# State reads of an attention block: the product computed transposed at once

## The chip, the cores and the metric

The kernel runs on one core of a Trainium2 chip. The metric is the device time of one launch in microseconds (us), as the median of the runs. The core has a matrix engine (TensorE, PE in the profile; its weight loads are shown as a lane of their own, PEld), VectorE (DVE), ScalarE (ACT), GpSimd (POOL) and a queue that issues DMAs (SP).

## The reference, cut to what matters

```python
# x (8, 8, 512, 64), state (8, 8, 32, 64), all float32
scores2 = scale * np.matmul(state, x.transpose(0, 1, 3, 2))
a2 = softmax(scores2)                      # (8, 8, 32, 512)
sread = np.matmul(a2, x)                   # (8, 8, 32, 64): the state reads
xread = np.matmul(softmax(scale * x @ state^T), state)
h = concat([xread, sread], axis=2)         # then to (8 * 544, 512)
h = (sigmoid(h @ w_gate) * (h @ w_val)) @ w_out
out = np.square(np.maximum(h @ w_in, 0)) @ w_out2
```

The change is in how `sread` is made: for each batch and head, 32 rows of probabilities over 512 tokens times the head's 512 x 64 slice of x.

## The kernel before

Every float32 operand of a product is split into a high and a low part of type fp32r (`h` and `l`), and a product is the sum of high x high, high x low and low x high (`mm3`, lines 182 to 184). PSUM holds sums in float32.

The work falls into three stretches. In the first, weights are converted, the states are multiplied by the first layer's weights (`state_weights`, `ps_g`), and the scores and the probabilities of the token reads are made (part A of the attention, tiles `ps_s`, `a`). In the second, the first feed-forward layer runs over the tokens: 96 units, one for each block of 512 tokens and each 128 of the hidden features (`front_x` with `psg` and `psv`, `back1` with `acc`), and part B of the attention, the state reads, is woven into it. It closes with 12 units for the 256 state rows (`front_s`). In the third, the second layer runs (`px`, `py`, `pz`, `o`).

Part B goes over 8 batches and 2 groups `g` of 4 heads, so 16 groups. A group holds heads in pairs: index `c` (or `p`) and index `i`, 4 heads in all. Its steps are named: LN loads x by tokens (`xn`), LS loads the scores (`e2`), B4 makes the softmax, B5 transposes the probabilities to tokens on partitions and splits them into `et` (128 tokens, 4 blocks of tokens, c, high or low, 64 state rows of two heads), SX0 and SX1 split x into `xs` (ACT casts the high part, POOL subtracts), B60 and B61 multiply, and B7 brings the result to its place. The result has to lie in `xs_t` with features on partitions, since `split_states` (tile `sp`) and `front_s` read it that way.

In B60 and B61 the loaded operand is `et`: 4 matmuls, one for each block of 128 tokens, with 128 loaded columns (high and low of 64 state rows) and 256 streamed columns (high and low of two heads of x). The output has the high rows in partitions 0 to 63 and the low rows in 64 to 127. ACT copies the lower half to `tmp`, DVE adds the upper half and then adds the two parts of x into `sw`. When both halves of `sw` are there, B7 transposes it on PE (`ps_so`) and picks the 4 blocks of 64 x 32 that belong together, 2 by DVE and 2 by ACT, into `xs_t`.

The order is that of emission. `ORDER_B` lists part B's steps with blanks, and each batch's list is laid evenly over 5.4 units from unit 45 + 5b on (`spread(att_b[b], start, start + 5.4)`); `step()`, called 6 times in a unit, emits what is due. The order on each engine is then refined when the program is built, by readiness on a simulated timeline, so that steps can come out later than their place in the list. The pool `at` has two PSUM banks, for `ps_e`, `ps_sr`, `ps_so`, `ps_g` and `ps_s` in turn; `xs`, `xn`, `et` and `sw` have one buffer each.

Of the kernel before, what the change touches and what calls it, by code (L numbers as in the profile page):

```python
# [8 lines left out]
F32 = mybir.dt.float32  # L9
F32R = mybir.dt.float32r  # L10
# [8 lines left out]
P = 128  # L19
# [13 lines left out]
def kernel(  # L33
# [12 lines left out]
    nc = tc.nc  # L46
    B, H, S, D = x.shape
    NS = state.shape[2]
# [8 lines left out]
    NT = S // P  # L57
# [18 lines left out]
    at_p = ctx.enter_context(tc.tile_pool(name="at", bufs=2, space=PSUM))  # L76
# [13 lines left out]
    xs_t = xs_p.tile([P, KD, NSTATE], F32, name="xs_t")  # L90

    ident = pad_p.tile([P, P], F32, name="ident")
# [108 lines left out]
    f_p = att.enter_context(tc.tile_pool(name="f2k", bufs=2))  # L201
# [42 lines left out]
    loaded_x, loaded_xn = {}, {}  # L244
# [37 lines left out]
    def group_stages(b, g):  # L282

        v = {}
# [10 lines left out]
        def a2(p):  # L295
            def run():
                if by_pe:
                    xf = at_p.tile([P, S], F32, tag="at", name="ps_xt")
                    for t in range(NT):
                        ts = slice(t * P, (t + 1) * P)  # L300
                        nc.tensor.transpose(xf[:, ts], loaded_x[b, g][:, p, t, :], ident)
                else:
                    xf = f_p.tile([P, S], F32, tag="xf", name="xf", bufs=1)
                    nc.vector.transpose(xf, loaded_x[b, g][:, p, :])
                h = xx_p.tile([P, S], F32R, tag="xth", name="xth")
                l = xx_p.tile([P, S], F32R, tag="xtl", name="xtl")
                nc.scalar.copy(out=h, in_=xf)
                nc.vector.tensor_sub(out=l, in0=xf, in1=h.bitcast(F32))
                v["xt", p] = (h, l)

            return run
# [67 lines left out]
            )  # L379
            v["et"] = et  # L380

        def sx(p):
            def run():
                xn = loaded_xn[b, g][:, :, NT * p : NT * (p + 1), :]
                xs = f_p.tile([P, 2, 2, NT, D], F32R, tag="xs", name="xs", bufs=1)
                nc.scalar.copy(out=xs[:, 0], in_=xn)
                nc.gpsimd.tensor_sub(out=xs[:, 1], in0=xn, in1=xs[:, 0].bitcast(F32))
                v["xs", p] = xs

            return run  # L390

        def b6(p):
            def run():
                et, xs = v["et"], v.pop(("xs", p))
                ps = at_p.tile([P, 512], F32, tag="at", name="ps_sr")
                pv = ps[:, : 4 * D]
                for t in range(NT):
                    nc.tensor.matmul(
                        pv,
                        et[:, t, p].rearrange("p l n -> p (l n)"),  # L400
                        xs[:, :, :, t, :],
                        start=(t == 0),
                        stop=(t == NT - 1),
                    )
                tmp = f_p.tile([64, 2, P], F32, tag="tmp", name="tmp", bufs=1)
                if p == 0:
                    v["w"] = f_p.tile([P, P], F32, tag="sw", name="sw", bufs=1)
                sv = pv.rearrange("p (l m) -> p l m", l=2)
                nc.scalar.copy(out=tmp, in_=sv[64:128])
                nc.vector.tensor_add(out=tmp, in0=sv[:64], in1=tmp)  # L410
                nc.vector.tensor_add(
                    out=v["w"][64 * p : 64 * (p + 1)], in0=tmp[:, 0, :], in1=tmp[:, 1, :]
                )

            return run

        def b7():
            w = v.pop("w")
            ps = at_p.tile([P, 2, 64], F32, tag="at", name="ps_so")
            nc.tensor.transpose(ps.rearrange("p a b -> p (a b)"), w, ident)  # L420
            for p in range(2):
                for i in range(2):
                    to = xs_t[D * p : D * (p + 1), 2 * g + i, b * NS : (b + 1) * NS]
                    src = ps[D * i : D * (i + 1), p, NS * i : NS * (i + 1)]
                    if i:
                        nc.scalar.copy(out=to, in_=src)
                    else:
                        nc.vector.tensor_copy(to, src)

        return {  # L430
            "LX": lx, "LN": ln, "LS": ls, "A20": a2(0), "A21": a2(1), "A3": a3, "A4": a4, "SX0": sx(0), "SX1": sx(1),
            "B4": b4, "B5": b5, "B60": b6(0), "B61": b6(1), "B7": b7,
        }

    ORDER_A = "LX.0 - - - A20.0 A21.0 LX.1 A3.0 - A4.0 - A20.1 A21.1 A3.1 - A4.1".split()

    ORDER_B = (
        "LN.0 LS.0 - - - B4.0 SX0.0 - B5.0 LS.1 - B60.0 SX1.0 LN.1 - B61.0 B4.1 SX0.1 - B5.1 "
        "B7.0 - B60.1 SX1.1 - B61.1 - B7.1"
    ).split()  # L440

    def attention(b):
        gs = [group_stages(b, g) for g in range(2)]
        pick = lambda names: [
            (lambda: None) if n == "-" else gs[int(n[-1])][n[:-2]] for n in names
        ]
        return [lambda: prep_diag(b), *pick(ORDER_A)], pick(ORDER_B)
# [542 lines left out]
    for b in range(QB, B):  # L990
        start = 33 + 7 * (b - QB)
        spread(att_a[b], start, start + 7)
    for b in range(B):
        start = 45 + 5 * b
# [39 lines left out]
    for i, (b, f, lo, hi) in enumerate(units):  # L1034
        count[0] = STEPS * i
        g = (front_x if b < B else front_s)(b, f)
# [73 lines left out]
```

## Time and profile before

| | |
|---|---|
| Median of 3 runs | 1500.55 us (1496.91 to 2657.24) |
| Profiled execution | 1500.54 us, span 1498.8 us |
| PE busy | 1431.0 us, 95% of the span |
| DVE, ACT, POOL busy | 940.2, 748.8 and 246.0 us |
| Granted TensorE clock, mean | 0.985 of full speed |

The span goes from the first to the last instruction of the core; the profiled time has 1.7 us around it. Busy time is the union of an engine's instructions. Matmuls are pipelined: the shown duration of one is longer than its distance to the next, and it is the distance, from start to start, that fills the engine's time.

### The profile page before, as it was taken

The page shows a single profiled execution, that of the slowest core. Times are in us where ns is not written, and L with a number is a line of the kernel's source. Part 1 is how long each engine was busy: PE and PEld are TensorE (multiplying, and loading weights), DVE is VectorE, ACT ScalarE, POOL GpSimd, SP SyncE. Part 2 cuts the span into 40 slices and gives each one's busy share as a digit, 9 for nine tenths or more (in the row PEclk, how much of TensorE's full clock was granted, in tenths as well). Part 3 has the DMA queues.
Part 4 walks back from the last instruction along what each step waited for, and adds up shares of the span by engine and source line. Part 5 has one row for each costly group of instructions (what it writes and reads, how often), then busy time and mean ns, then how long its engine had stood idle before and what let it go on. Part 6 is the DMA issues. An engine that isn't in the chain of part 4 may idle for free.

```text
span 1498.8 us, 19379 instructions
## 1 busy us (share of the span) xinstructions
PE 1431.0 (95%) x6552; PEld 1176.9 (79%) x6552; DVE 940.2 (63%) x1579; ACT 748.8 (50%) x1291; POOL 246.0 (16%) x216
## 2 busy tenths in 40 slices
PE   5879999999999989999899999999999999999998
PEld 3558878887787677888798788888888888888887
DVE  7986887578889987555536655734575356433443
ACT  6865876456678887666424522332242223232211
POOL 1112213232344544333101100000000000000000
PEclk9889999999999999999999999999999999999999
DMA  9984799699999864333677844644365443645442
GB/s 265 341 263 120 229 328 339 210 363 292 323 296 286 254 211 145 95 113 92 242 271 250 274 158 147 217 146 143 133 227 188 151 152 134 222 124 195 155 145 80
DMA packets 244595, 311.68 MB, mean 208 GB/s; under 512 B 105361, under 2 KB 152977, under 8 KB 244497
## 3 DMA queue, kind: packets, MB, share of 16 engines
q1 hardware_dynamic: 242224, 309.66, 63.8%
q10 hardware_dynamic: 2272, 0.79, 0.3%
q8 instruction: 52, 0.85, 0.2%
q14 instruction: 47, 0.38, 0.1%
HBM read 221.25 MB, written 89.13 MB: 207 GB/s over the span
## 4 chain that ended last, share of the span: by engine, by line
PE 72%; DVE 10%; ACT 7%; DMA 7%; issue 3%; SPq 1%; POOL 0%; ACTq 0%; DVEq 0%; POOLq 0%
PE o L182 8%; PE o L183 8%; PE o L184 8%; PE px L183 4%; PE px L182 4%; PE px L184 4%; PE acc L183 4%; PE acc L184 3%; PE acc L182 3%; DMA raw<-in_moe_w_out_dram 2%; PE psg L182 2%; PE psg L183 2%; PE psg L184 2%; PE psv L182 2%; PE psv L183 2%
## 5 line engine op out<-in xcount | busy, mean ns | idle before, releaser
L182 PE MATMUL o<-wo,g2h 128*128 128x512 f32 x512 | 198.6, 390 | 3.7 <-DMA wo<-wo 3.0
L183 PE MATMUL o<-wo,g2h 128*128 128x512 f32 x512 | 199.1, 389 | 0.0
L184 PE MATMUL o<-wo,g2l 128*128 128x512 f32 x512 | 193.9, 389 | 0.0
L537 POOL TENSOR_TENSOR gg<-gi,gg 128x512 fp32r<-128x512 f32 x96 | 135.3, 1412 | 350.5 <-ACT gg L536 284.2
L183 PE MATMUL acc<-gl,o 128*128 128x512 f32 (+1 forms) x432 | 164.4, 381 | 3.7 <-DVE gl L190 3.7
L184 PE MATMUL acc<-gh,o 128*128 128x512 f32 (+1 forms) x432 | 163.0, 378 | 0.0
L841 ACT CAST g2h<-c 128x512 fp32r<-128x512 f32 x96 | 59.3, 622 | 178.8 <-DVE c L837 178.8
L182 PE MATMUL acc<-gh,o 128*128 128x512 f32 (+1 forms) x432 | 139.3, 380 | 0.6 <-DVE y L624 0.4
L893 DVE TENSOR_TENSOR y<-o,y 128x512 f32<-128x512 f32 x102 | 68.5, 688 | 103.5 <-PE o L184 102.8
L182 PEld LDWEIGHTS o<-wo,g2h 128*128 128x128 f32 x512 | 96.1, 188 | 24.9 <-ACT p L826 3.0
L184 PEld LDWEIGHTS o<-wo,g2l 128*128 128x128 f32 x512 | 96.1, 188 | 19.8
L183 PEld LDWEIGHTS o<-wo,g2h 128*128 128x128 f32 x512 | 96.2, 188 | 19.5
L190 DVE TENSOR_TENSOR gl<-g,gh 128x512 fp32r<-128x512 f32 (+1 forms) x108 | 88.4, 818 | 36.3 <-ACT gh L189 35.8
L182 PE MATMUL px<-xh,wi 128*128 128x512 f32 x256 | 99.8, 390 | 0.0
L183 PE MATMUL px<-xl,wi 128*128 128x512 f32 x256 | 99.7, 389 | 0.0
L184 PE MATMUL px<-xh,wi 128*128 128x512 f32 x256 | 99.6, 389 | 0.0
L183 PEld LDWEIGHTS acc<-gl,o 128*128 128x128 f32 x432 | 81.3, 188 | 21.3 <-DVE gl L190 6.9
L182 PEld LDWEIGHTS acc<-gh,o 128*128 128x128 f32 x432 | 80.6, 189 | 17.4 <-DVE y L624 1.1
L184 PEld LDWEIGHTS acc<-gh,o 128*128 128x128 f32 x432 | 81.3, 188 | 14.6
L182 PE MATMUL psg<-a,gg 128*128 128x512 f32 x192 | 78.6, 409 | 14.8 <-ACT sg L550 12.1
L556 DVE TENSOR_TENSOR g<-psv,sg 128x512 f32<-128x512 f32 x96 | 65.6, 683 | 35.4 <-PE psv L184 21.6
L189 ACT CAST gh<-g 128x512 fp32r<-128x512 f32 (+1 forms) x108 | 64.3, 596 | 40.4 <-DVE g L556 23.0
(188 smaller groups left out, 3268.7 us busy)
## 6 DMA issues: line engine op xcount, KB each, us to landing
wi<-wi SPq DMA_DIRECT2D x256, 256.0 KB, 3.1
wo<-wo SPq DMA_DIRECT2D x64, 512.0 KB, 5.5
gd<-go SPq DMA_DIRECT2D x192, 128.0 KB, 4.4
gi<-gd SPq DMA_DIRECT2D x96, 256.0 KB, 4.0
wi<-wa SPq DMA_DIRECT2D x32, 512.0 KB, 5.0
wd<-w SPq DMA_DIRECT2D x24, 512.0 KB, 5.1
ws<-wd SPq DMA_DIRECT2D x24, 512.0 KB, 6.7
raw<-in_moe_w_out_dram SPq DMA_DIRECT2D x20, 512.0 KB, 6.2
```

The lines of the kernel that those rows point to most:

```text
L182: nc.tensor.matmul(ps, lh, rh, start=start, stop=False, skip_group_check=more)
L183: nc.tensor.matmul(ps, lh, rl, start=False, stop=False, skip_group_check=more)
L184: nc.tensor.matmul(ps, ll, rh, start=False, stop=stop, skip_group_check=more)
L189: nc.scalar.copy(out=gh[:, :n], in_=g32[:, :n])
L190: nc.vector.tensor_sub(out=gl[:, :n], in0=g32[:, :n], in1=gh[:, :n].bitcast(F32))
L537: nc.gpsimd.tensor_sub(out=t[:, 1], in0=src, in1=t[:, 0].bitcast(F32))
L556: nc.vector.tensor_mul(out=g32, in0=ps, in1=sg)
L841: nc.scalar.copy(out=h, in_=c)
L893: nc.vector.tensor_add(out=y, in0=acc, in1=y)
```

## The change

B60 and B61 now go by `i` instead of `p`. The loaded operand is the split x (128 tokens x 128 columns: two heads `c`, 64 features each), once for its high and once for its low part, and `et` is streamed: 128 columns, which are c, high or low, and the 32 state rows of head `i`. A step so has 8 matmuls of 128 streamed columns in place of 4 of 256. High and low of x are summed in PSUM. The output has features on partitions, as `xs_t` wants it; of its columns, those of the other head `c` are not used. ACT copies the low columns of the probabilities to `tmp` (128 x 64), and DVE adds the high columns to it in two additions of 64 x 32 that write to `xs_t`. B7, with its transposition and its four copies, and the tile `sw` are gone. `tmp` has two buffers of 128 x 64 instead of one of 64 x 256. `xs` holds the same numbers in another order. `ORDER_B` loses its two B7 steps and a blank: 25 entries in place of 28, over the same 5.4 units.

```diff
-        def sx(p):
+        def sx(i):
             def run():
-                xn = loaded_xn[b, g][:, :, NT * p : NT * (p + 1), :]
-                xs = f_p.tile([P, 2, 2, NT, D], F32R, tag="xs", name="xs", bufs=1)
+                xn = loaded_xn[b, g][:, i].rearrange("p (c t) d -> p t c d", c=2)
+                xs = f_p.tile([P, 2, NT, 2, D], F32R, tag="xs", name="xs", bufs=1)
                 nc.scalar.copy(out=xs[:, 0], in_=xn)
                 nc.gpsimd.tensor_sub(out=xs[:, 1], in0=xn, in1=xs[:, 0].bitcast(F32))
...
-        def b6(p):
+        def b6(i):
             def run():
-                et, xs = v["et"], v.pop(("xs", p))
-                ps = at_p.tile([P, 512], F32, tag="at", name="ps_sr")
-                pv = ps[:, : 4 * D]
+                et, xs = v["et"], v.pop(("xs", i))
+                rows = slice(NS * i, NS * (i + 1))
+                ps = at_p.tile([P, 2, 2, NS], F32, tag="at", name="ps_sr")
                 for t in range(NT):
-                    nc.tensor.matmul(
-                        pv,
-                        et[:, t, p].rearrange("p l n -> p (l n)"),
-                        xs[:, :, :, t, :],
-                        start=(t == 0),
-                        stop=(t == NT - 1),
+                    for l in range(2):
+                        nc.tensor.matmul(
+                            ps,
+                            xs[:, l, t].rearrange("p c d -> p (c d)"),
+                            et[:, t, :, :, rows],
+                            start=(t == l == 0),
+                            stop=(t == NT - 1 and l == 1),
+                        )
+                tmp = f_p.tile([P, 2, NS], F32, tag="tmp", name="tmp", bufs=2)
+                nc.scalar.copy(out=tmp, in_=ps[:, :, 1, :])
+                for p in range(2):
+                    half = slice(D * p, D * (p + 1))
+                    nc.vector.tensor_add(
+                        out=xs_t[half, 2 * g + i, b * NS : (b + 1) * NS],
+                        in0=ps[half, p, 0, :], in1=tmp[half, p, :],
                     )
-                tmp = f_p.tile([64, 2, P], F32, tag="tmp", name="tmp", bufs=1)
-                if p == 0:
-                    v["w"] = f_p.tile([P, P], F32, tag="sw", name="sw", bufs=1)
-                sv = pv.rearrange("p (l m) -> p l m", l=2)
-                nc.scalar.copy(out=tmp, in_=sv[64:128])
-                nc.vector.tensor_add(out=tmp, in0=sv[:64], in1=tmp)
-                nc.vector.tensor_add(
-                    out=v["w"][64 * p : 64 * (p + 1)], in0=tmp[:, 0, :], in1=tmp[:, 1, :]
-                )
...
-        def b7():
-            w = v.pop("w")
-            ps = at_p.tile([P, 2, 64], F32, tag="at", name="ps_so")
-            nc.tensor.transpose(ps.rearrange("p a b -> p (a b)"), w, ident)
-            for p in range(2):
-                for i in range(2):
-                    to = xs_t[D * p : D * (p + 1), 2 * g + i, b * NS : (b + 1) * NS]
-                    src = ps[D * i : D * (i + 1), p, NS * i : NS * (i + 1)]
-                    if i:
-                        nc.scalar.copy(out=to, in_=src)
-                    else:
-                        nc.vector.tensor_copy(to, src)
...
     ORDER_B = (
         "LN.0 LS.0 - - - B4.0 SX0.0 - B5.0 LS.1 - B60.0 SX1.0 LN.1 - B61.0 B4.1 SX0.1 - B5.1 "
-        "B7.0 - B60.1 SX1.1 - B61.1 - B7.1"
+        "- B60.1 SX1.1 - B61.1"
     ).split()
```

## Rows read from the trace of the kernel before

**Rows 1.** The page's first part: busy time, share of the span, instructions.
```profile
PE 1431.0 (95%) x6552; PEld 1176.9 (79%) x6552; DVE 940.2 (63%) x1579; ACT 748.8 (50%) x1291; POOL 246.0 (16%) x216
```
**Rows 2.** Busy time by windows; columns: stretch, length, engines, granted clock, DMA share, GB/s.
```profile
413.00:570.00 157.00, 144.70 (x636) 114.27 (x635) 139.25 (x243) 127.43 (x217) 76.92 (x62) 0.98 0.86 260
...
413.00:734.00 321.00, 304.36 (x1390) 246.21 (x1388) 234.31 (x427) 239.48 (x413) 134.11 (x105) 0.99 0.62 184
```
**Rows 3.** PE's waits from 413 to 735 us: us in total, times, longest.
```profile
PE psg L182 <- ACT sg L550: 6.8, 7, 3.0
PE ps_so L420 <- DVE sw L411: 2.9, 2, 1.5
```
**Rows 4.** Timeline of PE, 685 to 690 us: start, us, engine, line, tiles.
```profile
685.30 0.39 PE L182 MATMUL psg<-a,gg 128*128 128x512 f32 x1
...
687.12 0.39 PE L184 MATMUL psv<-a,gg 128*128 128x512 f32 x1
687.34 0.64 PE L398 MATMUL ps_sr<-xs,et 128*128 128x256 f32 x4
687.82 0.60 PE L373 MATMUL ps_e<-ident,e 128*128 128x128 f32 x4
688.17 0.48 PE L182 MATMUL acc<-gh,o 128*128 128x512 f32 x1
688.49 0.39 PE L183 MATMUL acc<-gl,o 128*128 128x512 f32 x1
```
**Rows 5.** Timeline of the weight loads in the same stretch.
```profile
687.72 0.46 PEld L373 LDWEIGHTS ps_e<-ident,e 128*128 128x128 f32 x4
688.14 0.19 PEld L182 LDWEIGHTS acc<-gh,o 128*128 128x128 f32 x1
688.25 0.19 PEld L183 LDWEIGHTS acc<-gl,o 128*128 128x128 f32 x1
```
**Rows 6.** Timeline of PE, 693 to 695 us: one transposition of B7.
```profile
693.74 0.28 PE L420 MATMUL ps_so<-ident,sw 128*128 128x128 f32 x1
693.77 0.94 PE L182 MATMUL acc<-gh,o 128*128 128x512 f32 x3
694.55 0.39 PE L183 MATMUL acc<-gl,o 128*128 128x512 f32 x1
```
**Rows 7.** Groups by line and shape, 413 to 735 us: busy us, mean ns | idle before.
```profile
L411 DVE TENSOR_TENSOR sw<-tmp 64x128 f32<-64x128 f32 x32 | 19.4, 607 | 0.9
...
L410 DVE TENSOR_TENSOR tmp<-ps_sr,tmp 64x256 f32<-64x256 f32 x32 | 13.2, 411 | 14.3 <-ACT tmp L409 14.2
...
L409 ACT COPY tmp<-ps_sr 64x256 f32<-64x256 f32 x32 | 11.8, 370 | 4.6 <-PE ps_sr L398 4.0
...
L426 ACT COPY xs_t<-ps_so 64x32 f32<-64x32 f32 x32 | 5.8, 182 | 10.8 <-DVE xs_t L428 10.2
L428 DVE COPY xs_t<-ps_so 64x32 f32<-64x32 f32 x32 | 5.8, 180 | 7.2 <-ACT xs_t L426 3.7 <-PE ps_so L420 3.2
...
L420 PE MATMUL ps_so<-ident,sw 128*128 128x128 f32 x16 | 4.4, 277 | 2.9 <-DVE sw L411 2.9
```
**Rows 8.** Timeline, 726 to 741 us: the end of part B and the first unit of the state rows.
```profile
730.16 0.64 PE L398 MATMUL ps_sr<-xs,et 128*128 128x256 f32 x4
...
731.82 0.28 DVE L411 TENSOR_TENSOR sw<-tmp 64x128 f32<-64x128 f32 x1
732.25 0.30 PE L420 MATMUL ps_so<-ident,sw 128*128 128x128 f32 x1 [1.45 <-DVE sw L411]
...
734.05 0.18 ACT L426 COPY xs_t<-ps_so 64x32 f32<-64x32 f32 x1
...
735.87 0.48 PE L182 MATMUL psg<-sp,ws 128*128 128x256 f32 x1 [3.32 <-ACT sp L564]
```
**Rows 9.** Busy time by windows behind that point (PE, PEld, DVE, ACT, POOL; the clock).
```profile
736.00:740.00 4.00, 3.27 (x14) 2.97 (x15) 2.45 (x4) 0.86 (x2) 0.00 (x0) 0.50 1.01 382
740.00:744.00 4.00, 4.00 (x20) 3.70 (x19) 0.85 (x2) 0.79 (x2) 0.00 (x0) 0.65 1.06 354
```

More of the change, by code (lines that the diff above doesn't have):

```diff
@@ L380, in b5 @@
             v["et"] = et
-        def sx(p):
+        def sx(i):
             def run():
-                xn = loaded_xn[b, g][:, :, NT * p : NT * (p + 1), :]
-                xs = f_p.tile([P, 2, 2, NT, D], F32R, tag="xs", name="xs", bufs=1)
+                xn = loaded_xn[b, g][:, i].rearrange("p (c t) d -> p t c d", c=2)
+                xs = f_p.tile([P, 2, NT, 2, D], F32R, tag="xs", name="xs", bufs=1)
                 nc.scalar.copy(out=xs[:, 0], in_=xn)
                 nc.gpsimd.tensor_sub(out=xs[:, 1], in0=xn, in1=xs[:, 0].bitcast(F32))
-                v["xs", p] = xs
+                v["xs", i] = xs
@@ L430, in group_stages @@
+                tmp = f_p.tile([P, 2, NS], F32, tag="tmp", name="tmp", bufs=2)
[5 more added lines that the diff above has]
+                        in0=ps[half, p, 0, :], in1=tmp[half, p, :],
+                    )
+            return run
         return {
             "LX": lx, "LN": ln, "LS": ls, "A20": a2(0), "A21": a2(1), "A3": a3, "A4": a4, "SX0": sx(0), "SX1": sx(1),
-            "B4": b4, "B5": b5, "B60": b6(0), "B61": b6(1), "B7": b7,
+            "B4": b4, "B5": b5, "B60": b6(0), "B61": b6(1),
```

## The prediction

> **What bounds the kernel now.** I began with the busy shares. PE is busy for 1431 us of the span [rows 1], so a microsecond added to or taken from PE's stream counts almost in full, while one of another engine counts only where PE waits for it. Next I cut the span at part B's first and last product and read the busy time by windows. In the 321 us from 413 to 734 PE is busy for 304.4 and idle for 16.6; DVE is busy for 234.3 and ACT for 239.5. In the first half of it, 413 to 570, DVE is at 139.3 of 157, and PE has 12.3 of its 16.6 idle us there [rows 2]. So the stretch is bound by PE, and in its first half DVE is close behind. PE's waits then say for whom it idles: most of all for ACT's sigmoid (6.8 us), then for DVE's `sw`, ahead of B7's transposition (2.9 us in two places) [rows 3]. The last view is the timeline of PE around single products, because in a pipelined engine the cost of a matmul is its distance to the next start and not its shown duration. That distance is where this change is decided.
>
> **The paces on PE.** From 685.30 to 687.12 lie 8 distances of 512-column matmuls, so 0.2275 us each. The 4 matmuls of `ps_sr`, with 256 columns, take from 687.34 to 687.82: 0.48 us, 0.12 each. The 4 transpositions behind them have 128 columns each, as the new products will, and a new loaded operand each: from 687.82 to the second matmul after them, at 688.49, it is 0.67, less one 512-column distance 0.44, so 0.11 each [rows 4]. That is more than their columns should take: going from 512 columns to 256 saves 0.1075 us, so another 128 fewer would give 0.0665. The lane of weight loads says why. The loads of the 4 transpositions begin at 687.72 and the next one at 688.14, 0.105 apart, and that next one, the load of an fp32r operand for `acc`, is followed by another at 688.25, 0.11 later [rows 5]. Behind 512 or 256 columns a load of 0.11 is hidden; behind 128 it isn't. The trace has no fp32r product with 128 columns, so this pace is my reading of its nearest rows: 0.11, between 0.0665 (columns alone) and 0.2275 (no faster than 512 columns, the far end).
>
> A rule of the Trainium skill differs from this reading. Its page "TensorE: Matmul & The Clock Gate", under "Back-to-back issue gap", gives about 81 ns for a sustained pair of weight load and 128-column matmul. No run here shows such a pace; by it a step would take 0.65 us and the total would come out some 7 us lower than below.
>
> **The change part by part.**
>
> The products. There are 32 steps B60 and B61 [rows 7] (the copies of L409). Each has 8 pairs by 0.11, 0.88 us, in place of 0.48: +0.40. The last of the 32 lies at the end of part B and is counted there, so 31 x 0.40 = +12.4 us, all on the path, since PE is the bound. With 0.12 a pair it would be 14.9, with 0.0665 1.6, with 0.2275 41.5. That `et` is now streamed in runs of 32 numbers instead of 64 I cost at nothing; no row shows such a stream, and the bounds of the pace cover it.
>
> The transpositions. One of them with 3 matmuls of 512 takes from 693.74 to 694.55, 0.81 less 0.68, so 0.13 us [rows 6]. Of 16 [rows 7], one lies at the end: 15 x 0.13 = -2.0 us.
>
> The wait for `sw`. Of its 2.9 us [rows 3] 1.45 lie at the end of part B [rows 8]; the other 1.4 goes as well, because PE no longer waits for this sum in the middle of its stream. What is late next there is the ordinary next matmul, which has its operands. -1.4 us.
>
> DVE and ACT. For one step DVE had 411 (sum to `tmp`) + 607 (`sw`) + 180 (one of the 32 copies) = 1198 ns, and ACT 370 + 182 = 552 [rows 7]. Now DVE has two additions of 64 x 32 from PSUM. The nearest row is the copy of that shape at 180; a sum can take longer, and the PSUM sum of 64 x 256 at 411 is its upper end. I take 180, because L410 and L428 both read PSUM and differ mainly in columns: 360 ns for both. ACT copies 128 x 64: between 182 (32 columns) and 370 (256 columns) the slope is 0.84 ns a column, so 209. Over 32 steps DVE loses 26.8 us of work and ACT 11.0. Neither is the bound, so these don't come off the time; they come off PE's waits for queued DVE and ACT work. What PE's idle leaves without the two waits for `sw` (2.9) and the 1.4 us already idle for the state rows before 734 is 12.3 us. The relief is 11% of DVE's work in the stretch and 5% of ACT's [rows 2]. I take a fifth of 12.3: -2.5 us, with bounds of 0 (the waits are for PE's own results going round through ACT) and -12.3. The wait of DVE for ACT's `tmp` (14.3 us of DVE's time, rows 7) stays: the additions still need it. The copies that wait for each other in B7 (10.2 us of ACT's time) go, but nobody on PE waited for them except at the end.
>
> The end of part B. Here the chain is bare. The last product starts at 730.16; `sw` ends at 732.10; then come the transposition and four copies in turn on DVE and ACT, the last of which ends at 734.23; then `split_states` makes `sp`, and PE starts the state rows at 735.87, after idling for 1.45 and 3.32 [rows 8]. The change takes out the piece from 732.10 to 734.23, 2.13 us. The work before it gets shorter by 370 + 411 + 280 - 209 - 360 = 492 ns and longer by the product's 0.40. Together -2.2 us. What is late next is `sp` itself, which stays. After that idle stretch the granted clock is 0.50 from 736 to 740 and 0.65 from 740 to 744, half speed for part of it; PE loses about 3.27 x 0.5 + 4 x 0.35 = 3.0 us there [rows 9]. With an idle stretch of some 2.5 us instead of 4.8 the clock may not fall. I leave the 3.0 us in the sum, for the idle time stays, and keep them for the range.
>
> What costs nothing. `xs` is split with the same number of elements on ACT and POOL. No DMA is added or removed, and none changes its size. The list of part B has 25 entries over the same 5.4 units, so its last product is due at 24/25 x 5.4 = 5.18 units instead of 25/28 x 5.4 = 4.82, a third of a unit later; behind it stand no transposition and no copies any more. The cover is PE's own stream: a product that comes later lets feed-forward matmuls go first. Only at the end is there no such cover; if another step falls behind the last token unit, the bare chain from 730.16 to 735.87 comes twice, which is +5.7 us at most.
>
> The sum: +12.4 - 2.0 - 1.4 - 2.5 - 2.2 = +4.3 us. It is made against the profiled execution, 1500.54 us, which is the median of the runs shown to a hundredth. That gives **1505 us**. Its own range, with 0.12 a pair and no relief at the top and a relief of 8 more us at the bottom, is 1497 to 1510. A change of 2%, 30 us, is about what a measurement of this kernel can tell from none.
>
> **The rivals.**
>
> *Slower: the narrow fp32r product runs at the pace of the wide one.* If 128 streamed columns take as long as 512 do, 0.2275 a pair, the products cost +41.5 and the end of part B saves 1.3 instead of 2.2: +41.5 - 2.0 - 1.4 - 2.5 - 1.3 = +34.3, 1535 us. For it: every fp32r product in the trace has 256 or 512 columns, and no row shows that the type stays at one column a cycle below that. Against it: 256 columns already run at twice the pace of 512. It decides from 0.093 us a pair on, where the sum turns from gain to loss (31 x (8p - 0.48) = 8.1), and takes the time over 2% from 0.213 on.
>
> *Faster: the weight load hides.* If loads run further ahead than one and the pair goes at its columns, 0.0665, the products cost only +1.6 and the total is -6.5, 1494 us. Against it stand the loads that follow each other at 0.105 to 0.11 [rows 5]. The Trainium skill's 81 ns (the section named above) lies between the two and would give some 1498 us.
>
> *Faster: the relief is worth more.* DVE at 139.3 of 157 us in the first half [rows 2] is a queue, and in a queue near its limit a ninth less work can remove most of the waiting. All 12.3 us and the clock's 3.0: 1505 - 9.8 - 3.0 = 1492 us. Against it: the largest wait is for the sigmoid [rows 3], which stands on ACT, and ACT loses only 5%.
>
> *Part B falls further behind.* One more step at the bare end: 1511 us.
>
> *The change doesn't do what it says.* The chain behind the product is as long as before, since DVE waits for ACT's `tmp` as it did. Then only the relief is missing, 1507 us, inside the forecast's range.
>
> **How the numbers follow.** I give the forecast 0.60 (with the case that the relief is missing), the slow narrow product 0.20, the hidden load 0.08, the large relief 0.08, and the later part B 0.04. The range reaches from 1490 to 1530: it takes in the forecast, the hidden load, most of the large relief, the later part B, and paces up to 0.21 of the slow product, about a third of that case. Left out are some 0.16. Slower by over 2% means over 1530.6 us, two thirds of the slow case: 0.13. Faster by over 2% would need 30 us, and all gains together make some 21: 0.01. Within 2%: 0.86.
>
> **What would show it.** In the changed kernel's timeline the 8 matmuls of one `ps_sr` should span 0.88 us from start to the next tile's start, with the loads 0.11 apart; 0.53 would mean hidden loads, 1.8 the slow product. The groups by line should have the two DVE additions near 180 ns and the ACT copy near 209, and DVE's busy time from first to last product should fall by some 27 us. PE's idle time there should be near 11 us. Between the last `ps_sr` and the first `psg` of the state rows there should be some 3.5 us instead of 5.7. The prediction is wrong above all if the pace of a pair is, and it would be wrong through the order if more part B steps than two stand behind the last token unit.

## The result and the profile after

| | before | after |
|---|---|---|
| Median | 1499.78 us (4 runs) | 1513.35 us (4 runs, 1512.29 to 1520.62) |
| Profiled execution | 1500.54 us, span 1498.8 | 1512.52 us, span 1510.7 |
| PE, DVE, ACT busy | 1431.0, 940.2, 748.8 us | 1440.5, 923.7, 731.7 us |

The ratio is 1.0103, 95% interval 1.0084 to 1.0123: the changed kernel is 1% slower. That lies inside 2% and inside the predicted range, but 8 us above the forecast of 1505. One run of before, at 2657 us, was disturbed and is left out of the ratio; the median of the other three is 1499.02. Of the change itself more is missing than those 8 us: forecast were +4.3, and the ratio makes +15.4. The base of the forecast, 1500.54, lay 1.5 us above that median, which hides part of it.

The first part of the page of after, to be read against [rows 1]:

```profile
PE 1440.5 (95%) x6664; PEld 1186.0 (79%) x6664; DVE 923.7 (61%) x1547; ACT 731.7 (48%) x1259; POOL 244.9 (16%) x216
```

PE has 9.5 us more to do, in 112 more matmuls (32 x 4 more, less 16 transpositions). DVE and ACT have 16.5 and 17.1 us less. That is the change as written: work goes from the engines that don't bound the kernel to the one that does.

PE's timeline of after around one step, start and shown duration in us, to be read against [rows 4]:

```profile
679.20 0.39 PE L184 MATMUL psg<-a,gg 128*128 128x512 f32 x1
679.42 1.00 PE L399 MATMUL ps_sr<-et,xs 128*128 128x128 f32 x8
680.26 0.45 PE L182 MATMUL psv<-a,gg 128*128 128x512 f32 x1
680.55 0.40 PE L183 MATMUL psv<-a,gg 128*128 128x512 f32 x1
...
738.77 1.07 PE L182 MATMUL acc<-gh,o 128*128 128x512 f32 x4
739.68 0.27 PE L182 MATMUL psg<-sp,ws 128*128 128x256 f32 x1
...
743.23 0.39 PE L182 MATMUL psg<-sp,ws 128*128 128x256 f32 x1 [0.84 <-DMA ws<-wd]
...
745.79 0.38 PE L182 MATMUL psg<-sp,ws 128*128 128x256 f32 x1 [1.58 <-DMA ws<-wd]
...
748.36 0.58 PE L182 MATMUL psg<-sp,ws 128*128 128x256 f32 x1 [1.60 <-DMA ws<-wd]
```

The weight loads of after beside the same step, against [rows 5]:

```profile
679.20 1.08 PEld L399 LDWEIGHTS ps_sr<-et,xs 128*128 128x128 f32 x8
680.20 0.19 PEld L182 LDWEIGHTS psv<-a,gg 128*128 128x128 f32 x1
680.32 0.19 PEld L183 LDWEIGHTS psv<-a,gg 128*128 128x128 f32 x1
```

From the first of the 8 matmuls at 679.42 to the second matmul behind them at 680.55, less one 512-column distance of 0.2275, is 0.90 us: 0.112 a pair. The first of the 8 loads still lies beside the matmul before, at 679.20; from it to the next tile's load it is 1.00 us, and one more load follows 0.12 later. The narrow fp32r product runs neither at its columns nor at the wide product's pace, but at that of its loads.

The lower half of the timeline is the end of part B, against [rows 8]. The wait for `sp` is gone: the first `psg` of the state rows at 739.68 follows `acc` without idle time. But its next three steps, 2.56 us apart, each wait for weights `ws`. Why, the queue's own timeline shows. SP issues the 8 loads of `ws` here, in after:

```profile
736.29 4.10 SPq L557 DMA_DIRECT2D ws<-wd  x8
```

and here, in before:

```profile
724.29 3.84 SPq L570 DMA_DIRECT2D ws<-wd  x8
```

In before the first state product comes 11.6 us after the issue (735.87); in after it comes 3.4 us after it. Of the 8.2 us between the two, 5.7 are part B's last step and its bare chain, which in before lie ahead of that product, and some 2.5 are an issue that comes later in PE's stream of token matmuls. The long end of part B had been most of the cover of these loads. Each is 512 KB, so at the 398 GB/s that the DMAs move from 745 to 749 (below) two of them would take 2.6 us, about the distance of the three steps.

PE's waits in after from 411 to 737 us, against [rows 3], and from 735 to 880 us behind "...": us in total, times, longest.

```profile
PE psg L182 <- ACT sg L537: 7.0, 5, 2.2
PE acc L183 <- DVE gl L190: 5.0, 7, 1.3
PE acc L182 <- ACT gh L189: 1.3, 2, 1.0
...
PE psg L182 <- DMA ws<-wd: 4.0, 3, 1.6
PE o L182 <- DMA wo<-wo: 3.9, 1, 3.9
```

`sw` is gone from the list, but `gl` has gone from 1.0 us in before to 5.0. Busy time of after by windows, against [rows 2, 9] (PE, PEld, DVE, ACT, POOL, then clock, DMA share, GB/s):

```profile
411.00:570.00 159.00, 144.75 (x674) 114.36 (x673) 142.10 (x242) 125.08 (x211) 73.27 (x61) 1.00 0.83 259
...
413.00:734.00 321.00, 303.45 (x1455) 246.40 (x1454) 223.57 (x404) 226.27 (x389) 133.51 (x105) 1.00 0.59 179
...
745.00:749.00 4.00, 1.62 (x9) 1.41 (x10) 0.00 (x0) 0.00 (x0) 0.00 (x0) 0.71 1.03 398
749.00:753.00 4.00, 4.00 (x19) 3.81 (x19) 0.85 (x2) 0.86 (x3) 0.00 (x0) 0.50 0.96 309
...
860.00:880.00 20.00, 17.37 (x70) 14.22 (x71) 11.23 (x18) 8.58 (x15) 1.29 (x1) 0.91 0.75 274
```

PE is idle for 17.6 us from 413 to 734. In before it was 16.6, of which 2.9 belonged to the end of part B; so the middle of the stretch has 17.6 in place of 13.7. Not all of that is the change. The run before_in_order (below) has before's steps in this stretch, yet its PE idles for 16.5 us, at a clock of 1.00 as in after and not at before's 0.99:

```profile
416.00:733.00 317.00, 300.53 (x1381) 242.36 (x1380) 231.76 (x419) 236.21 (x407) 134.48 (x105) 1.00 0.62 182
```

Against it the rise is 1.1 us. After the waits for `ws` the granted clock is 0.50, the lower of its two levels (1.2 GHz), from 749 to 753, as it was in before behind the wait for `sp`. And PE waits 3.9 us for `wo` at 862.63, 50 us into the second layer, with a clock of 0.91 from 860 to 880; in before two waits for `wo` come to 3.0.

Groups by line and shape in after, 411 to 740 us, to be read against [rows 7] (busy us, mean ns | idle before):

```profile
L410 DVE TENSOR_TENSOR xs_t<-ps_sr,tmp 64x32 f32<-64x32 f32 x64 | 11.9, 186 | 16.5 <-ACT tmp L407 16.0
L399 PE MATMUL ps_sr<-et,xs 128*128 128x128 f32 x256 | 34.5, 268 | 2.1 <-DVE et L377 1.3 <-POOL xs L387 0.8
L407 ACT COPY tmp<-ps_sr 128x64 f32<-128x64 f32 x32 | 6.6, 207 | 6.0 <-PE ps_sr L399 5.8
```

The shown durations of the 256 products (268 ns) overlap; their distance, 112 ns, is what PE pays.

### The profile page after: what moved, and what is told of

Read it like the earlier page. It is cut to its first block, busy times and chain, and to the rows that moved or that the text cites. A ratio compares the mean times of both kernels' runs of the same rounds, so it can differ in the third digit from the quotient of the medians.

```text
span 1510.7 us, 19521 instructions
## 1 busy us (share of the span) xinstructions
PE 1440.5 (95%) x6664; PEld 1186.0 (79%) x6664; DVE 923.7 (61%) x1547; ACT 731.7 (48%) x1259; POOL 244.9 (16%) x216
## 4 chain that ended last, share of the span: by engine, by line
PE 68%; DVE 11%; DMA 9%; ACT 6%; issue 3%; SPq 1%; POOL 0%; ACTq 0%; DVEq 0%; POOLq 0%
PE o L182 8%; PE o L183 8%; PE o L184 8%; PE px L182 4%; PE px L183 4%; PE px L184 4%; PE acc L183 3%; PE acc L184 3%; PE acc L182 3%; PE psg L182 2%; PE psg L183 2%; PE psg L184 2%; PE psv L182 2%; PE psv L183 2%; PE pz L183 2%
## 5 line engine op out<-in xcount | busy, mean ns | idle before, releaser
L184 PE MATMUL acc<-gh,o 128*128 128x512 f32 (+1 forms) x432 | 163.7, 379 | 0.0
L182 PE MATMUL acc<-gh,o 128*128 128x512 f32 (+1 forms) x432 | 141.7, 380 | 2.0 <-ACT gh L189 1.3
```

What stands on the lines that cost most here:

```text
L182: nc.tensor.matmul(ps, lh, rh, start=start, stop=False, skip_group_check=more)
L184: nc.tensor.matmul(ps, ll, rh, start=False, stop=stop, skip_group_check=more)
```

## Experiments

The theory after the result: the products cost what their loads cost, some 13 us; B7's removal gives less than forecast; and the end of part B waits for `ws` instead of `sp`. Rivals were that the products cost something else (streaming short runs of `et`, shape), or that the loss lies in the new order of steps alone. Each ratio is against runs of before on the same chip (medians 1499.6 to 1500.2); 0.1% is 1.5 us.

| run | median us | ratio, 95% interval |
|---|---|---|
| after | 1513.35 | 1.0103 [1.0084, 1.0123] |
| x_high_only | 1502.93 | 1.0016 [1.0007, 1.0026] |
| stream_64 | 1518.87 | 1.0130 [1.0104, 1.0156] |
| old_product | 1496.88 | 0.9978 [0.9961, 0.9995] |
| weights_in_order | 1508.41 | 1.0053 [1.0035, 1.0070] |
| old_product_in_order | 1493.16 | 0.9961 [0.9944, 0.9979] |
| before_in_order | 1499.21 | 0.9998 [0.9983, 1.0013] |
| stream_256 | 1516.58 | 1.0111 [1.0088, 1.0135] |
| before_earlier | 1516.58 | 1.0108 [1.0089, 1.0127] |
| before_split | 1497.37 | 0.9982 [0.9970, 0.9995] |

**x_high_only: half of the products.**

```diff
-                    for l in range(2):
+                    for l in range(1):
...
-                            stop=(t == NT - 1 and l == 1),
+                            stop=(t == NT - 1),
```

> The changed kernel with only the high part of x loaded, so 4 pairs of load and 128-column matmul a step in place of 8 (the low part of x is left out of the sums). Theory (the pairs are the whole cost, 0.11 us each, and the waits elsewhere only change places): 32 x 4 x 0.11 = 14.1 us less than the changed kernel's 1513.4, so 1499, with a ps_sr step of 0.46 us on PE. Rival (the products cost what they should, but most of the loss comes from the new order and the new wait for weights behind the last token unit): at least 1507.

PE's timeline in it:

```profile
693.33 0.56 PE L399 MATMUL ps_sr<-et,xs 128*128 128x128 f32 x4
693.73 0.45 PE L184 MATMUL acc<-gh,o 128*128 128x512 f32 x1
694.02 0.40 PE L182 MATMUL psg<-a,gg 128*128 128x512 f32 x1
```

694.02 - 0.2275 - 693.33 = 0.46 us a step, half of 0.90. The 32 steps are so worth 14.1 us; between the ratios lie 0.87%, 13 us, between the medians 10.4. The extra pairs are the cost, and nearly all of it is on the path. The median stayed 4 us above the 1499 expected.

**stream_64: half of the streamed columns, the same loads.**

```diff
-                            ps,
+                            ps[:, :, 0, :],
                             xs[:, l, t].rearrange("p c d -> p (c d)"),
-                            et[:, t, :, :, rows],
+                            et[:, t, :, 0, rows],
...
-                nc.scalar.copy(out=tmp, in_=ps[:, :, 1, :])
+                nc.scalar.copy(out=tmp, in_=ps[:, :, 0, :])
```

> The changed kernel with only the high part of the probabilities streamed: 8 pairs of 64 columns instead of 128, loads unchanged (the low part of the probabilities is left out). Theory (the weight load paces the pair): 0.11 us a pair as before, 1513 us within 2. Rival (the narrow fp32r matmul itself paces it, at half the speed of a wide one: 128 columns in 0.107): 0.06 us a pair, 32 x 8 x 0.05 = 12.8 us less, 1501.

PE's timeline in it:

```profile
630.03 0.97 PE L399 MATMUL ps_sr<-et,xs 128*128 128x64 f32 x8
630.84 0.48 PE L182 MATMUL psv<-a,gg 128*128 128x512 f32 x1
631.16 0.40 PE L183 MATMUL psv<-a,gg 128*128 128x512 f32 x1
```

631.16 - 0.2275 - 630.03 = 0.90 us: the same with 64 columns as with 128. The rival, a price by columns, is refuted. The columns alone take less: the second of the 8 matmuls starts at 630.06, 0.03 us behind the first, and in after at 679.48, 0.06 behind; only from there on do the starts follow at the loads' 0.11. That it came out 5.5 us slower than after (4.0 by the ratios, whose intervals overlap) neither theory expected. It has the same pace of products and 20.5 us of idle PE in the stretch instead of 17.6; the refined order differs. I take this as the size of the shifts that a new order can bring by itself, and rely on differences below 5 us only where a row shows them.

**stream_256: twice the columns.** All of `et[:, t]` is streamed, both heads `i`, of which one is used.

```diff
...
-                            et[:, t, :, :, rows],
+                            et[:, t],
...
```

> The changed kernel with both heads' rows streamed in each step: 8 pairs of 256 columns in place of 128, half of the output unused. Theory (a pair costs the load's 0.11 until the columns take longer, 0.12 at 256): 32 x 8 x 0.01 = 2.6 us more than the changed kernel, 1516. Rival (columns streamed cost time in proportion): 0.22 us a pair and 28 us more, 1541.

PE's timeline in it:

```profile
679.77 1.11 PE L399 MATMUL ps_sr<-et,xs 128*128 128x256 f32 x8
680.73 0.40 PE L182 MATMUL psv<-a,gg 128*128 128x512 f32 x1
680.96 0.40 PE L183 MATMUL psv<-a,gg 128*128 128x512 f32 x1
```

The next tile starts 0.96 us after the first, 0.12 a pair. Twice the streamed columns cost 7% of a step. In the next tile the two matmuls stand 0.23 apart, the ordinary distance, where behind 128 columns it was 0.29: behind 256 columns the load is hidden again. Columns are nearly free up to 256; loads are not.

**old_product: after, with before's form of product and without B7.**

```diff
...
-                    for l in range(2):
-                        nc.tensor.matmul(
-                            ps,
-                            xs[:, l, t].rearrange("p c d -> p (c d)"),
-                            et[:, t, :, :, rows],
+                    nc.tensor.matmul(
+                        wide,
+                        et[:, t, i].rearrange("p l n -> p (l n)"),
+                        xs[:, :, t],
...
```

> The changed kernel with the product of the kernel before (4 matmuls, et loaded, 256 columns of x streamed); copies, additions, step list and the lack of B7 as in the changed kernel (the numbers summed are not those that belong together). Theory (beyond the transpositions, the removal of B7 and of DVE work is worth next to nothing, since PE's waits change places): 32 x 0.41 = 13.1 us less than the changed kernel, 1500, the time of the kernel before. Rival (the relief of 6 us that was forecast is real and hidden behind another loss in the changed kernel): 1494 or less.

PE's waits in it from 411 to 737 us:

```profile
PE psg L182 <- ACT sg L538: 6.3, 7, 1.6
PE acc L183 <- DVE gl L190: 4.6, 5, 1.9
PE psg L182 <- DMA ws<-wd: 4.1, 2, 2.5
```

The median fell by 16.5 us against after, between what the theory (1500) and the rival (1494 or less) expected. Against before, B7's removal and the lighter copies are worth 0.22%, 3.3 us, and that is little more than the 16 transpositions alone (16 x 0.13 = 2.1). Here too `gl` has taken the place of `sw`, and the wait for `ws` stands at the end (5.6 us in three waits, the third behind 737): both come without the new product. The exchange for `gl` hangs on the refined order as well, for stream_256, with the DVE and ACT work of after, waits only 1.7 us for it.

**weights_in_order: the loads of `ws` in the order of their use.** The 8 loads alternate between the two halves of the hidden features; the first state unit needs only one half, so each of its steps waits for two loads. One term in the key sorts them.

```diff
-                spread([lambda ch=ch, c=c: load_gv(ch, c)], max(i - 3, u_s - 0.4) + c / 50, i)
+                spread([lambda ch=ch, c=c: load_gv(ch, c)], max(i - 3, u_s - 0.4) + ch / 10 + c / 50, i)
```

> The changed kernel with only the order of 8 weight loads altered: the four for the first two units of the state rows go ahead of the four for the next two, instead of alternating. Theory (at the end of part B the wait for sp was replaced by a wait for these weights, 4.0 us of idle PE and half the clock for some 5 us behind it): 4 to 7 us less, 1507 to 1509. Rival (the next thing is late at the same place, or the stall is hidden anyway): 1513.

PE's waits in it, and the windows behind the first state rows (columns as above):

```profile
PE psg L182 <- DMA ws<-wd: 0.2, 1, 0.2
```

```profile
744.00:748.00 4.00, 4.00 (x25) 3.44 (x24) 1.38 (x2) 1.17 (x2) 0.00 (x0) 1.00 0.99 389
748.00:752.00 4.00, 3.64 (x29) 3.23 (x28) 0.85 (x2) 0.90 (x3) 0.00 (x0) 1.00 1.02 412
```

The wait fell from 4.0 to 0.2 us, the clock stayed at 1.00, and the time fell by 4.9 us by the medians, 7.5 by the ratios. No byte less is moved.

**old_product_in_order and before_in_order: the same line in old_product and in before.**

> The kernel of the run old_product (product of the kernel before, without B7; the numbers summed are not those that belong together), with the weights of the state rows in order. Theory (the forecast gain at the end of part B is real, but the wait for the weights takes its place): the 5.6 us of idle PE for ws and the half clock behind it go, 5 to 7 us less than old_product's 1496.9, so 1490 to 1492. Rival (removing B7 is worth only its transpositions, whatever is late at the end): 1496.

> The kernel before with only the weights of the state rows in order. Theory (there the end waits for sp, behind which the weights are hidden): the time of the kernel before, 1499.6 within 1.5. Rival (the weights were late there too): 4 us or more less.

PE's wait at the end of part B in before_in_order, and then in old_product_in_order:

```profile
PE psg L182 <- ACT sp L564: 3.3, 1, 3.3
```

```profile
PE psg L182 <- DMA ws<-wd: 2.9, 1, 2.9
```

In before the line is worth nothing, for there the wait for `sp` (3.3 us, as in [rows 8]) ends last whatever the weights do. In old_product it gives 3.7 us by the medians, 2.6 by the ratios (their intervals overlap), and leaves 2.9 of waiting, so less than expected. The end is the later of two arrivals, `sp` and `ws`; shortening one is worth something up to the other.

**before_earlier: before with the loads in order and all of part B four units earlier.** If the bare end is the cost, an earlier part B should remove it.

```diff
-        start = 45 + 5 * b
+        start = 41 + 5 * b
```

> The kernel before with the weights in order and part B begun 4 units earlier (unit 41 + 5b instead of 45 + 5b); products and B7 as in the kernel before. Theory (both waits at the end of part B are gone, 5.5 us of idle PE and some 3 us of half clock, with no change of the product): 1491 to 1494, the fastest correct version. Rival (part B begun earlier collides with the weight preparation in the first half, where DVE is at nine tenths): 1498 or more.

Windows of before_earlier and then of before:

```profile
452.00:500.00 48.00, 35.20 (x144) 27.56 (x143) 38.84 (x78) 34.18 (x60) 16.88 (x16) 0.84 0.87 279
```

```profile
452.00:500.00 48.00, 44.42 (x190) 34.43 (x189) 46.04 (x78) 41.41 (x70) 25.44 (x23) 0.96 0.93 283
```

My theory (1491 to 1494) fell; it is 17 us slower than before. In the stretch where part B now starts earlier, PE is busy for 35.2 of the 48 us instead of 44.4, at a clock of 0.84 instead of 0.96, and what comes back at the end is less. That part B there meets part A and the first units is the likely reason; which engine holds PE up was not separated.

**before_split: before with a shorter bare chain.** In order as above, and `split_states` in four pieces, so that PE can start on the first 128 features.

```diff
-        nc.scalar.copy(out=t[:, 0], in_=xs_t)
-        nc.vector.tensor_sub(out=t[:, 1], in0=xs_t, in1=t[:, 0].bitcast(F32))
+        for k in range(KD):
+            nc.scalar.copy(out=t[:, 0, k], in_=xs_t[:, k])
+            nc.vector.tensor_sub(out=t[:, 1, k], in0=xs_t[:, k], in1=t[:, 0, k].bitcast(F32))
```

> The kernel before with the weights of the state rows in order and split_states cut into four pieces, one for each 128 features, so that the first units of the state rows need not wait for all of xs_t. Theory (the end of part B waits for sp alone once the weights are in order; half of xs_t is ready one product earlier): part of the 4.8 us of idle PE goes, and the half clock behind it with it, 3 to 6 us less than the kernel before, 1494 to 1497. Rival (the pieces cost DVE and ACT at this place what they save, or PE waits for the last piece as long): 1499 or more.

PE's timeline in it at the end of part B, and the window behind it:

```profile
729.24 0.28 PE L182 MATMUL psg<-sp,ws 128*128 128x256 f32 x1
...
731.35 0.33 PE L420 MATMUL ps_so<-ident,sw 128*128 128x128 f32 x1
733.84 0.39 PE L182 MATMUL psg<-sp,ws 128*128 128x256 f32 x1 [2.16 <-ACT sp L565]
```

```profile
736.00:740.00 4.00, 3.95 (x19) 3.66 (x18) 1.96 (x4) 0.79 (x2) 0.00 (x0) 0.50 0.99 321
```

The first state products now come at 729.24, ahead of the last product of part B and its transposition. From the last transposition to the next state product it takes 2.49 us, where in before it took 3.62 to the first [rows 8]. The median is 2.8 us below before's, the ratio 0.18% (0.05 to 0.30): the fastest of these versions that computes the whole reference, though the clock still falls to 0.50 behind the shorter wait.

## Why the prediction was right in kind and 8 us low

**What bounds the kernel, and the pace of a pair: right.** Forecast 0.88 us a step and +12.4 us, measured 0.90; 32 steps by 0.90 - 0.48 = 0.42 are +13.4. (The 0.90 is taken for all 32; where other matmuls stand among the 8, a step can cost less.) With the load order set right in both, the change of product alone (weights_in_order against old_product_in_order) is 0.92% or 13.8 us. That the load sets the pace was argued from the transpositions; x_high_only, stream_64 and stream_256 show it: half the pairs cost half, half or twice the columns cost nothing or 7%.

**Rivals on the pace: refuted.** 0.2275 a pair (1535 us) and 0.0665 (1494 us) are both off. The narrow product as such is not slow: the first distance in a step, 0.06 us behind 128 columns and 0.03 behind 64 (stream_64, above), is about what the prediction had for columns alone. For the 81 ns that the Trainium skill gives in "TensorE: Matmul & The Clock Gate", "Back-to-back issue gap", no run here shows a stream of this type that reaches it: measured are 112 ns. The same page's rule under "LDWEIGHTS (loading the stationary operand)", columns divided by 1.2 for the ns of a load, makes 107 ns for 128 columns, and with that the traces agree to within 5 ns.

**The transpositions: consistent.** -2.0 forecast; no run isolates them, but old_product's 3.3 us below before have room for 2.1.

**The wait for `sw` (-1.4) and the relief (-2.5): nothing of them came.** The sizes of the operations were right: additions 186 ns (forecast 180), copy 207 (209), and DVE's removed operations are 38.4 us [rows 7] against 11.9 added, -26.5 (-26.8). Yet PE's idle time in the middle of the stretch did not fall by 3.9 us: it went from 13.7 to 17.6, or from 16.5 to 17.6 with the clock at 1.00 in both (before_in_order). The wait did not go, it moved: `sw` 1.4 less, `gl` 4.0 more. In old_product, which has the same DVE and ACT operations as after, it moved likewise, so no run but stream_256 (14.9 us idle, from 412 to 740) shows that freeing DVE and ACT bought PE any time. The step that "the ordinary next matmul has its operands" failed: the next one was as often an `acc` whose `gl` DVE had not finished. Most of the rise against before was paid back by the clock, 1.00 over 413 to 734 where it had been 0.99 [rows 2], which is up to 3 us of PE's work.

**The end of part B (-2.2): this is the step that failed most.** It said "what is late next is `sp` itself, which stays". The wait for `sp` vanished altogether, as part B's last product ended at 704.85, 31 us before the last `psv` of the tokens (735.82), and not a third of a unit later as the list had it. The build's refinement put it there, in old_product as well; why, no run tells. So the end gave 5.7 us, the 5.9 from the last token matmul to the first state product less the 0.2 that stay, and not 2.2. Next late were the weights `ws`, a DMA that stood in none of the prediction's rows, because in before it had 11.6 us of cover. They bring 4.0 us of waiting and the clock's fall to 0.50 again. The wait for `wo` is 0.3 us in weights_in_order, but that it hangs on `ws` is not shown: old_product waits 5.6 us for `ws` and none for `wo`. weights_in_order gives back 4.9 us (7.5 by the ratio), about half or more of what the forecast missed.

**The ledger.** By the ratios: removing B7 with its copies, loads in order in both, gives -0.37% (before_in_order to old_product_in_order), -5.5 us, where I had -8.1 for the last four terms together. The new product gives +13.8 for +12.4. The load order gives +7.5 for 0, less 0.3 that it gives in before. These are links of one chain from before to after, so they add up to after's own +15.4 whatever their noise; each has an uncertainty of 3 to 4 us, and stream_64 shows that reordering alone can move as much. The profiles say where the time lies, one execution of each kernel, starts in us:

| run | first `ps_sr` | first `psg<-sp` | between them | from there to the span's end |
|---|---|---|---|---|
| before | 413.58 | 735.87 | 322.3 | 762.9 |
| before_in_order | 415.92 | 739.02 | 323.1 | 764.0 |
| after | 411.41 | 739.68 | 328.3 | 771.0 |
| weights_in_order | 414.81 | 744.59 | 329.8 | 760.9 |

Up to the first state product after takes 6.0 us more than before, or 7.8 with 8 token matmuls (`acc`, 1.8 us) that in after come behind it; the whole forecast, +4.3, belonged here. Behind it after takes 8.1 us more, or 6.3 without those 8, where the forecast had nothing. In the first part two misses work against each other: the end gave 3.5 us more than forecast (less the last step's product, 0.9, which only moved ahead), and the missing relief, with the somewhat dearer product, took more than that back. That the total missed by no more is in part luck. So the cost of the `ws` loads at the end and the pace of a pair are shown; why the relief did not come, and how the last 2 to 3 us divide, stays open. The profile of after holds idle time before `gl`, but no run tells why the refined order put it there.

**Chances.** Two forms of slower were weighed: a slow pace (0.20) and one more step of part B at the end (0.04). The one that came is a third: a hidden transfer that loses its cover.

## What to carry to other kernels

When two operands can trade places, count the loads, not the flops: each new 128-column load costs PE about 0.11 us unless 256 or more columns stream behind it. Here x split is twice as wide as the probabilities, so loading it meant 8 pairs for 4, and +13 us on the bounding engine against 26 us less on one that was not. Before taking credit for shortening a chain in front of a bare wait, list every input of the instruction that waits, DMAs too, with its issue time: the gain ends at the second-latest of them. And count nothing for freeing an engine that is not the bound until a row shows who would have waited less.

## What was not expected of the hardware

fp32r pairs with 64 and with 128 streamed columns take the same 0.112 us, and 256 take 0.120, though the first distance of a step is 0.03 us behind 64 columns and 0.06 behind 128. PE's clock fell to 0.50 behind three waits of 0.84, 1.58 and 1.60 us close together (after) as it did behind 1.45 and 3.32 (before) and, in before_split, behind waits of which the longest was 2.16; behind a wait of 0.2 us it stayed at 1.00 (weights_in_order). DVE's busy time over the whole run fell by only 16.5 us for 26.5 us of removed work, so other operations took longer; one group, here in after and then in before, over the whole run:

```profile
L131 DVE CUSTOM_DVE_ANT_0 c<-c,q 128x1024 uint16<-128x1024 uint16 x72 | 59.4, 826 | 0.7
```

```profile
L131 DVE CUSTOM_DVE_ANT_0 c<-c,q 128x1024 uint16<-128x1024 uint16 x72 | 55.1, 767 | 0.7
```

Its code and shape are unchanged, and the mean went from 767 to 826 ns. Much of that can be spread between executions: before_in_order, with before's DVE operations, has 789, and the other runs lie from 768 (before_earlier) to 848 (old_product_in_order). What lengthens it stays open.
